# S4D convolution with a gated feed-forward layer: one of the multiplies that build the taps goes from VectorE to GpSimd, and the planner's rules and numbers change

## The chip, the cores and the metric

The kernel runs on one core of a Trainium2 chip. A core has TensorE (PE in the tables; PEld is its weight load), VectorE (DVE), ScalarE (ACT), GpSimd (POOL) and SyncE (SP), which here issues nearly all DMAs. The engines run side by side, each through its own instructions in a fixed order, and wait for each other by semaphores. SBUF is the on-chip memory that all of them work on; PSUM is the small memory that TensorE writes and that VectorE and ScalarE read. The metric is the device time of one execution in microseconds (us).

## The reference

Two branches over the same input `u` of 2048 positions by 640 channels are mixed by a gate. Branch A is a state-space layer: for each channel a kernel `K` of 2048 taps is a sum over 128 complex exponentials, and `u` is convolved with it (by an FFT in the reference). Branch B is a feed-forward layer with 1728 hidden units.

```python
def _A_ref(u, log_A_real, A_imag, C_real, C_imag, log_dt, D_skip):
    dt = jnp.exp(log_dt)
    A = -jnp.exp(log_A_real) + 1j * A_imag
    C = (C_real + 1j * C_imag) * dt[:, None]
    P = jnp.exp((A * dt[:, None])[:, :, None] * pos[None, None, :])
    K = 2.0 * jnp.einsum("dn,dnl->dl", C, P).real
    ...
    y = jnp.fft.irfft(Uf * Kf[None, :, :], L2)[:, :, :L]
    return y + u * D_skip[None, None, :]

def _B_ref(x, w1, w2):
    h = jnp.maximum(jnp.einsum("bsd,df->bsf", x, w1), 0)
    return jnp.einsum("bsf,fd->bsd", h, w2)

g = _sigmoid((x * gate_w).sum(-1, keepdims=True))
return g * a + (1 - g) * b
```

## The kernel before

**The branches.** The feed-forward layer runs as single-pass float32 matmuls of split operands (a high and a low half, `w1h`/`w1l`, `hh`/`hl`), into PSUM banks named `pf`, in three parts of the hidden units. The state-space layer has three stages: parameters (small vector work on 128x640 tables), generation of the taps, and the convolution as a two-level transform with matmuls into banks named `pc`. The feed-forward matmuls fill TensorE between the matmuls of the other branch through the whole run.

**Generation.** The 640 channels go in 40 chunks of 16, and two chunks make a pair. For a chunk of 128 states by 16 channels:

- TensorE multiplies the chunk's parameters with small tables into the only `pg` buffer (`products`, `pe`). The columns are phases in turns and logarithms of magnitudes, 64 of each per channel: 32 fine steps and 32 coarse ones.
- ScalarE rounds the phases to integers (`whole`, the CAST `sc<-pg`) and takes Exp of the magnitudes (`exps`, `mg<-pg`), VectorE subtracts the rounded phase (`sc<-pg,sc`) and clears the sign (`sc<-sc`, TENSOR_SCALAR), and ScalarE takes the Sine and the Cosine (`sc<-sc`, `sc<-sc,half_pi`). The subtraction is what frees `pg`, together with Exp.
- GpSimd sets a column of the magnitudes and extends them by one multiply of 128x512 (`long`: MEMSET `mg`, TENSOR_TENSOR `mg<-mg`).
- `factors` makes the factors of the tap matmuls by four multiplies: parts 0 and 1 (`G<-mg,sc`, 128x512 each), part 2 (`mg<-mg,sc`, 128x1024) and part 3 (`sc<-sc,mg`, 128x1024), which multiplies the fine sines and cosines, in place, by the fine magnitudes. All four read two tiles of SBUF.

The pair then goes through 64 small matmuls into `pk` (`taps`; the trace counts each as two), a transposition on VectorE (`kt<-pk`), a small addition on GpSimd (`kt<-kt,dsk`) and four stores. ScalarE takes the pair's steps in a fixed order, with a table load at each change between Exp and Sine.

**What sets the order.** The program isn't written in the order in which it runs. Each step is a task `A(engine, queue, duration, function, dependences, ...)` with a rank. `Plan.run` then plays the engines forward with the given durations: each engine takes, of the heads of its queues, the one that is ready with the lowest priority number. The priority is the rank plus a number from the table `moves`, by the task's index. The functions are called in the order so found, and `Pinned` keeps each engine's instructions in that order. So durations, rules and table change nothing but the order of instructions on every engine. `run` also counts blocks of 128 matmul instructions on TensorE: a block can begin only some time (`FETCH`, and more by `BUSY` while DMAs are under way) after the one before it. `port=True` lets a VectorE task take up to a quarter longer while the plan has GpSimd busy.

All the instructions go through one helper, so every row of the trace has the line 416; rows are told apart by tile names.

Of the kernel before, what the change touches and what calls it, by code (L numbers as in the profile page):

```python
# [133 lines left out]
def moves():  # L134
    r = {}
    for v, s in (
# [128 lines left out]
class Plan:  # L265
# [3 lines left out]
    CHANGE = dict(PE=0.15, ACT=1.3)  # L269
    HOLD = .1  # L270
    FETCH = 3.2
    BUSY = 0.4
    WAITS = 1.0095
    STALL = 3.0
    SLACK = .4
# [1313 lines left out]
```

## Time and profile before

| | us |
|---|---|
| median of 3 runs (673.36 to 676.02) | 673.42 |
| the profiled execution | 671.55 |
| its span, first to last instruction | 669.8 |
| VectorE busy | 535.4 |
| TensorE busy | 613.2 |
| ScalarE busy | 376.8 |
| GpSimd busy | 148.0 |

The granted clock of TensorE is 0.977 of full speed. In the profile's rows a group is `engine operation out<-in shapes xcount | busy us, mean ns | idle us just before, and what ended it`. A row in order of time begins with its start and its duration in us. "issue" is time in which an engine waited for nothing that the trace shows. A row of a tile gives shortest, median and longest duration in ns. A busy TensorE is not one at its peak, since its matmuls overlap.

### The profile page before, as it was taken

Reading aid. Unit: us, or ns where it says so; the run is one execution under the profiler, and the core shown is the slowest. Engines: PE = TensorE matmul, PEld = TensorE weight load, DVE = VectorE, ACT = ScalarE, POOL = GpSimd, SP = SyncE. Lnnn points to the kernel's source line nnn. Section 1 sums busy time; section 2 is a strip of 40 time slices with the busy share of each in tenths; the row PEclk is TensorE's granted clock in tenths of the full one; section 3 lists DMA queues with packets and bytes.
Section 4 is the critical chain, followed back from the end, with each engine's and each line's share of the span. In section 5 each row is a group of like instructions: output and inputs, shape, how many; then the busy total and the mean of one; then the engine's idle time right before and its main releaser. Section 6 shows DMA issues by size and latency. Waiting matters only on the chain.

```text
span 669.8 us, 19196 instructions
## 1 busy us (share of the span) xinstructions
PE 613.2 (92%) x8196; PEld 481.6 (72%) x8196; DVE 535.4 (80%) x778; ACT 376.8 (56%) x535; POOL 148.0 (22%) x213
## 2 busy tenths in 40 slices
PE   7988988898998999999999987997999997799985
PEld 6988978897886988987978866653675544546673
DVE  4899849999999899998989892987678676678441
ACT  5446378886998678887787860050532522333422
POOL 0000011112112222221322210050520621522633
PEclk9999999998999899998999997999999997999998
DMA  9955844232455552641742468654057837046345
GB/s 245 320 184 190 258 155 146 68 144 97 126 161 158 214 171 56 233 125 37 249 134 57 138 140 296 157 171 101 13 193 216 198 111 221 23 116 181 80 137 117
DMA packets 76302, 102.76 MB, mean 153 GB/s; under 512 B 7609, under 2 KB 59449, under 8 KB 75962
## 3 DMA queue, kind: packets, MB, share of 16 engines
q1 hardware_dynamic: 76058, 101.14, 50.2%
q8 instruction: 64, 1.05, 0.7%
q10 hardware_dynamic: 160, 0.41, 0.3%
q14 instruction: 20, 0.16, 0.1%
HBM read 62.33 MB, written 39.19 MB: 152 GB/s over the span
## 4 chain that ended last, share of the span: by engine, by line
PE 50%; DVE 20%; issue 11%; ACT 7%; DMA 6%; SPq 2%; POOL 2%; POOLq 0%; DVEq 0%; ACTq 0%
PE pf L416 33%; PE pc L416 10%; PE pk L416 5%; DVE sc L416 5%; ACT sc L416 3%; DVE G L416 3%; SPq L416 2%; PE pg L416 2%; DMA y__84<-yo 2%; DVE mg L416 2%; DVE ku L416 2%; DMA xu<-in_A_u_dram 2%; ACT mg L416 1%; POOL ku L416 1%; DVE hl L416 1%
## 5 line engine op out<-in xcount | busy, mean ns | idle before, releaser
L416 PE MATMUL pf<-xx,w1h 128*128 128x256 f32 (+1 forms) x760 | 190.1, 347 | 3.8 <-issue 1.3
L416 PEld LDWEIGHTS pf<-xx,w1h 128*128 128x128 f32 x760 | 124.8, 192 | 37.3 <-issue 22.2
L416 PE MATMUL pf<-xx,w1l 128*128 128x512 f32 (+1 forms) x340 | 117.1, 345 | 0.1
L416 PE MATMUL pf<-w2h,hh 128*128 128x320 f32 x288 | 91.2, 320 | 3.0 <-DVE q L416 1.5
L416 POOL TENSOR_TENSOR mg<-mg 128x512 f32<-128x512 f32 x40 | 51.9, 1298 | 177.1 <-ACT mg L416 177.1
L416 PE MATMUL pf<-w2l,hh 128*128 128x320 f32 x288 | 88.4, 311 | 0.0
L416 DVE STREAM_TRANSPOSE ku<-pc 128x512 f32<-128x512 f32 x80 | 76.1, 1061 | 6.3 <-PE pc L416 6.2
L416 ACT COPY ku<-pc 128x512 f32<-128x512 f32 (+1 forms) x60 | 43.7, 748 | 60.3 <-PE pc L416 60.1
L416 POOL TENSOR_TENSOR ku<-ku,kx 128x256 f32<-128x256 f32 x80 | 56.2, 736 | 92.9 <-DVE ku L416 69.8
L416 PE MATMUL pf<-w2h,hl 128*128 128x320 f32 x256 | 75.4, 318 | 0.8 <-DVE hl L416 0.8
L416 PEld LDWEIGHTS pf<-xx,w1l 128*128 128x128 f32 x340 | 65.3, 192 | 9.4 <-issue 1.5
L416 PEld LDWEIGHTS pf<-w2h,hh 128*128 128x128 f32 x288 | 54.6, 190 | 12.0 <-issue 5.2
L416 ACT CAST sc<-pg 128x1024 int32<-128x1024 f32 x40 | 40.5, 1012 | 39.8 <-PE pg L416 39.8
L416 DVE TENSOR_TENSOR sc<-pg,sc 128x1024 f32<-128x1024 f32 x40 | 48.7, 1217 | 9.6 <-ACT mg L416 9.3
L416 ACT ACT_TABLE_LOAD x42 | 53.9, 1283 | 2.7 <-PE pk L416 2.0
L416 PEld LDWEIGHTS pf<-w2l,hh 128*128 128x128 f32 x288 | 54.7, 190 | 0.2
L416 PEld LDWEIGHTS pf<-w2h,hl 128*128 128x128 f32 x256 | 46.9, 190 | 7.6 <-issue 6.1
L416 DVE TENSOR_TENSOR mg<-mg,sc 128x1024 f32<-128x1024 f32 x40 | 50.5, 1262 | 2.3
L416 ACT ACTIVATE hh<-pf 128x512 fp32r<-128x512 f32 (+1 forms) x40 | 20.4, 509 | 53.7 <-PE pf L416 53.6
L416 DVE TENSOR_TENSOR sc<-sc,mg 128x1024 f32<-128x1024 f32 x40 | 49.5, 1238 | 0.0
L416 PE MATMUL pc<-ku,tm 64*32 64x256 f32 x1280 | 43.4, 397 | 6.4 <-issue 4.2
L416 DVE STREAM_TRANSPOSE ku<-ku 128x512 f32<-128x512 f32 x40 | 25.5, 685 | 25.9 <-ACT ku L416 25.9
(165 smaller groups left out, 1182.2 us busy)
## 6 DMA issues: line engine op xcount, KB each, us to landing
xx<-xt SPq DMA_DIRECT2D x24, 640.0 KB, 5.5
xt<-xx SPq DMA_DIRECT2D x16, 640.0 KB, 5.5
part<-q SPq DMA_DIRECT2D x16, 640.0 KB, 3.4
q<-part SPq DMA_DIRECT2D x16, 640.0 KB, 4.3
ws<-in_B_w_dram SPq DMA_DIRECT2D x20, 320.0 KB, 3.9
kd<-kt SPq DMA_DIRECT2D x80, 64.0 KB, 1.8
ck<-kd SPq DMA_DIRECT2D x40, 128.0 KB, 2.8
xu<-in_A_u_dram SPq DMA_DIRECT2D x10, 512.0 KB, 5.9
```

What stands on the lines that cost most here:

```text
L416: return lambda *a, **k: self._tc.keep_in_program_order(f(*a, **k))
```

## The change

Part 3 of `factors` runs on GpSimd. In the planner, a VectorE, ScalarE or GpSimd task that follows one of its own engine that it depends on begins 0.11 later than it did (`RAW`); the request for a block of matmul instructions is made 24 instructions ahead of the block's start (`AHEAD`, through `when`), and no earlier than the task's dependences; `FETCH` and `BUSY` are larger. A number of durations are smaller, no task has `port=True` any more, and the table of `moves` is another one.

```diff
     for v, s in (
-            (-3.36, "588-683/5"),
+            (-2.99, "2"),
...
-    FETCH = 3.2
-    BUSY = 0.4
+    FETCH = 3.55
+    BUSY = 0.5
+    AHEAD = 24
+    RAW = 0.11
...
-                r = max(r, d.end - d.lag if d.eng == t.eng else d.end)
+                r = max(r, d.end - d.lag + (self.RAW if d.eng in ('DVE', 'ACT', 'POOL') else 0) if d.eng == t.eng else d.end)
...
+        def block():
+            return asked + self.FETCH + self.BUSY * min(12.0, max(0.0, dma - asked))
+
+        def when(c):
+            for (t0, a), (t1, b) in zip(ran[-2::-1], ran[:0:-1]):
+                if a <= c:
+                    return t0 + (t1 - t0) * (c - a) / (b - a) if b > a else t1
+            return 0.0
...
-                done += self.WAITS * t.n
+                w = self.WAITS * t.n
+                ran += [(start + change, total), (self.free[e], total + w)]
+                done, total = done + w, total + w
                 while done >= 128:
                     done -= 128
-                    at = self.free[e] - t.dur * min(1, done / t.n)
-                    self.free[e] += max(0, block - at)
-                    at = max(at, block)
-                    block = at + self.FETCH + self.BUSY * min(8.0, max(0.0, dma - at))
+                    c, at, b = total - done, self.free[e] - t.dur * min(1, done / w), block()
+                    if b > at:
+                        self.free[e] += b - at
+                        ran[-1:] = [(at, c), (b, c), (self.free[e], total)]
+                        at = b
+                    asked = min(at, max(known, when(c - self.AHEAD)))
...
-            y = A('POOL', 'm', 1.6, long, [x], use=[m_], rank=1)
+            y = A('POOL', 'm', 1.15, long, [x], use=[m_], rank=1)
...
                         x = st.pop(('s2', c))[:, :, :, :32]
-                        V.tensor_mul(x, x, m[:, None, :, 65:97].to_broadcast([128, 2, C, 32]))
+                        P.tensor_mul(x, x, m[:, None, :, 65:97].to_broadcast([128, 2, C, 32]))
...
             for k, dep in enumerate(((ex, sn), (ex, sn), (ex, cs), (me, sn, cs))):
-                fs.append(A('DVE', 'g4', 1.2 if k > 1 else 0.62, part(k), dep, take=[g_] if k == 0 else (),
-                            use=[w['s'], w['m']] + ([g_] if k == 1 else []), rank=G4R, port=True))
+                if k == 3:
+                    fs.append(A('POOL', 'f', 2.15, part(k), dep, use=[w['s'], w['m']], rank=G4R))
+                    break
+                fs.append(A('DVE', 'g4', 1.14 if k > 1 else 0.6, part(k), dep, take=[g_] if k == 0 else (),
+                            use=[w['s'], w['m']] + ([g_] if k == 1 else []), rank=G4R))
```

VectorE in the middle of the generation, at one pair of chunks, before (the numbers tell tiles apart: `sc_3360` and `sc_3405` are the two chunks' phases and sines, `sc_3547` belongs to the next pair; `q` is the feed-forward layer's sum, read from PSUM):

```order
L416 STREAM_TRANSPOSE kt_3507<-pk_3426 128x8x2x32
L416 SCALAR_TENSOR_TENSOR G_3513<-mg_3369,sc_3360 128x16x32
L416 TENSOR_TENSOR q_3121<-pf_3410,q_3121 128x320
L416 TENSOR_TENSOR G_3513<-mg_3369,sc_3360 128x16x32
L416 TENSOR_TENSOR mg_3369<-mg_3369,sc_3360 128x16x2x32
L416 TENSOR_TENSOR q_3121<-pf_3516,q_3121 128x320
L416 TENSOR_TENSOR sc_3360<-sc_3360,mg_3369 128x32x32
L416 SCALAR_TENSOR_TENSOR G_3563<-mg_3422,sc_3405 128x16x32
L416 TENSOR_TENSOR q_3121<-pf_3541,q_3121 128x320
L416 TENSOR_TENSOR G_3563<-mg_3422,sc_3405 128x16x32
L416 TENSOR_TENSOR sc_3547<-pg_3498,sc_3547 128x1024
```

And the same pair of chunks' place in the changed kernel (`sc_3293` and `sc_3341` are the pair, `sc_3464` the next pair's first chunk), as far as the next pair's subtraction:

```order
L444 STREAM_TRANSPOSE kt_3425<-pk_3343 128x8x2x32
L444 SCALAR_TENSOR_TENSOR G_3428<-mg_3302,sc_3293 128x16x32
L444 TENSOR_TENSOR G_3428<-mg_3302,sc_3293 128x16x32
L444 TENSOR_TENSOR q_2944<-pf_3334,q_2944 128x320
L444 TENSOR_TENSOR mg_3302<-mg_3302,sc_3293 128x16x2x32
L444 SCALAR_TENSOR_TENSOR G_3462<-mg_3408,sc_3341 128x16x32
L444 TENSOR_TENSOR q_2944<-pf_3438,q_2944 128x320
L444 TENSOR_TENSOR G_3462<-mg_3408,sc_3341 128x16x32
L444 TENSOR_TENSOR mg_3408<-mg_3408,sc_3341 128x16x2x32
L444 TENSOR_TENSOR q_3115<-pf_3466,q_3115 128x320
L444 TENSOR_TENSOR sc_3464<-pg_3415,sc_3464 128x1024
```

The multiplies `sc<-sc,mg` are gone from VectorE, and both chunks' `mg<-mg,sc` now stand ahead of the next pair's subtraction; before, the second chunk's followed it. One pair later VectorE has:

```order
L444 SCALAR_TENSOR_TENSOR G_3630<-mg_3478,sc_3464 128x16x32
L444 TENSOR_TENSOR G_3630<-mg_3478,sc_3464 128x16x32
L444 TENSOR_TENSOR mg_3478<-mg_3478,sc_3464 128x16x2x32
L444 TENSOR_TENSOR q_3115<-pf_3622,q_3115 128x320
L444 SCALAR_TENSOR_TENSOR G_3655<-mg_3589,sc_3577 128x16x32
L444 TENSOR_TENSOR G_3655<-mg_3589,sc_3577 128x16x32
L444 TENSOR_TENSOR mg_3589<-mg_3589,sc_3577 128x16x2x32
L444 TENSOR_TENSOR sc_3657<-pg_3617,sc_3657 128x1024
```

The order of the steps is the same, with one `q` among them. GpSimd in the changed kernel, at the first of these two pairs:

```order
L444 MEMSET mg_3302 128x16
L444 TENSOR_TENSOR mg_3302<-mg_3302 128x16x32
L444 MEMSET mg_3408 128x16
L444 TENSOR_TENSOR mg_3408<-mg_3408 128x16x32
L444 TENSOR_TENSOR kt_3425<-kt_3425,dsk_119 128x8
L444 TENSOR_TENSOR sc_3293<-sc_3293,mg_3302 128x32x32
L444 TENSOR_TENSOR sc_3341<-sc_3341,mg_3408 128x32x32
```

The last two rows are new there; before, the `kt` addition was followed by the next pair's MEMSET. TensorE at the start of the first block of the convolution, before (`pc<-ku,tm` are the small matmuls, `pf` the feed-forward ones):

```order
L416 MATMUL pc<-ku,tm 32x256 x48
L416 MATMUL pf<-xx,w1h_4513 128x512 x2
L416 MATMUL pf<-xx,w1l_4514 128x512
L416 MATMUL pc<-ku,tm 32x256 x32
L416 MATMUL pf<-xx,w1h_4513 128x512 x2
L416 MATMUL pf<-xx,w1l_4514 128x512
L416 MATMUL pc<-ku,tm 32x256 x48
```

and in the changed kernel:

```order
L444 MATMUL pc<-ku,tm 32x256 x48
L444 MATMUL pf<-xx,w1h_4418 128x512 x2
L444 MATMUL pf<-xx,w1l_4419 128x512
L444 MATMUL pc<-ku,tm 32x256 x16
L444 MATMUL pf<-xx,w1h_4418 128x512 x2
L444 MATMUL pf<-xx,w1l_4419 128x512
L444 MATMUL pc<-ku,tm 32x256 x32
L444 MATMUL pf<-xx,w1h_4418 128x512 x2
L444 MATMUL pf<-xx,w1l_4419 128x512
L444 MATMUL pc<-ku,tm 32x256 x32
```

The same 128 small matmuls stand in four runs where there were three.

More of the change, by code (lines that the diff above doesn't have):

```diff
@@ L268 @@
     LAG = dict(PE=0.22, DVE=0.12, ACT=0.12, POOL=0.1, SP=0.0, PY=0.0)
-    CHANGE = dict(PE=0.15, ACT=1.3)
+    CHANGE = dict(PE=0.12, ACT=1.3)
     HOLD = .1
-    FETCH = 3.2
-    BUSY = 0.4
+    FETCH = 3.55
+    BUSY = 0.5
+    AHEAD = 24
+    RAW = 0.11
     WAITS = 1.0095
@@ L332, in run @@
         self.free = {e: 0.0 for e in self.LAG}
-        mode, dma, log, done, block = {}, 0.0, [], 34.0, 3.0
+        mode, dma, log, done, total, asked, ran = {}, 0.0, [], 34.0, 34.0, -1.0, [(0.0, 34.0)]
         heads = {k: 0 for k in self.queues}
+        def block():
[5 more added lines that the diff above has]
+            return 0.0
         while True:
@@ L356, in key @@
                     if e == 'PE' and done + t.n >= 128:
-                        k += self.STALL * max(0.0, block - at - t.dur * (128 - done) / t.n)
+                        k += self.STALL * max(0.0, block() - at - t.dur * (128 - done) / t.n)
                     return k
@@ L373, in run @@
             _, e, t, start = best
+            known = self.ready(t)[0]
             change = self.CHANGE.get(e, 0) if t.mode is not None and mode.get(e) not in (None, t.mode) else 0
@@ L381, in run @@
             if e == 'PE':
-                done += self.WAITS * t.n
+                w = self.WAITS * t.n
+                ran += [(start + change, total), (self.free[e], total + w)]
+                done, total = done + w, total + w
                 while done >= 128:
                     done -= 128
-                    at = self.free[e] - t.dur * min(1, done / t.n)
-                    self.free[e] += max(0, block - at)
-                    at = max(at, block)
-                    block = at + self.FETCH + self.BUSY * min(8.0, max(0.0, dma - at))
+                    c, at, b = total - done, self.free[e] - t.dur * min(1, done / w), block()
[4 more added lines that the diff above has]
+                    asked = min(at, max(known, when(c - self.AHEAD)))
+                del ran[:-400]
             if t.port:
@@ L575, in logits @@
                 else:
-                    self.zs.append(A('DVE', 'z', 0.85, lambda t=t: go(t), dep, use=[s_], rank=LOGR))
+                    self.zs.append(A('DVE', 'z', 0.74, lambda t=t: go(t), dep, use=[s_], rank=LOGR))
         def trans(g, third, src):
@@ L842, in gates @@
             for k in range(17):
-                a = [A('DVE', 'gate', 0.2, rec.one(k, 17, go), a, rank=4)]
+                a = [A('DVE', 'gate', 0.16, rec.one(k, 17, go), a, rank=4)]
             self.gated = a[0]
@@ L1168, in long @@
                 P.tensor_mul(m[:, :, :32], m[:, :, 63:31:-1], m[:, :, 33:34].to_broadcast([128, C, 32]))
-            a = visit[c] = A('PE', None, 0.24, pe, [rd, opened, *self.tg_done], take=[p_], use=[r_], rank=GPR, mode='r', n=4)
+            a = visit[c] = A('PE', None, 0.28, pe, [rd, opened, *self.tg_done], take=[p_], use=[r_], rank=GPR, mode='r', n=4)
             b = acts[c, 0] = A('ACT', None, 0.97, whole, [a], take=[s_], use=[p_], rank=2)
@@ L1173, in products @@
                   use=[p_, s_], rank=G1R)
-            y = A('POOL', 'm', 1.6, long, [x], use=[m_], rank=1)
+            y = A('POOL', 'm', 1.15, long, [x], use=[m_], rank=1)
             o = A('DVE', 'g1', 0.62, lambda: V.tensor_scalar(I(st['sc', c][1]), I(st['sc', c][0]), 0x7fffffff, None,
-                                                             op0=ALU.bitwise_and), [d], use=[s_], rank=G1R, port=True)
+                                                             op0=ALU.bitwise_and), [d], use=[s_], rank=G1R)
             h = TWO_PI
@@ L1357, in stage1 @@
                 self.plan.join([pes[kind, i, q - 1], a])
-            ts = [A('DVE', 's' + kind, 1.04, turn(h), [a], use=[b_, buf], rank=SKD if k else SUD)
+            ts = [A('DVE', 's' + kind, 0.95, turn(h), [a], use=[b_, buf], rank=SKD if k else SUD)
                   for h in range(2)]
@@ L1428, in inv2 @@
                 gs = range(t * 4 // TURNS, (t + 1) * 4 // TURNS)
-                vs.append(A('PE', None, 1.76 / TURNS, lambda gs=gs: pe(gs), [*dep, tn] + vs[-1:], take=() if t else bs,
+                vs.append(A('PE', None, 1.8 / TURNS, lambda gs=gs: pe(gs), [*dep, tn] + vs[-1:], take=() if t else bs,
                             use=[K[i]] + (list(bs) if t else []), rank=S2P, mode='c', n=128 // TURNS))
@@ L1436, in relay @@
             d = slice(r * 8, r * 8 + 8)
-            return A('DVE', 'rl', 0.7, lambda: V.transpose(out=st['Y', i][:, :, d].rearrange("p b e f -> p e f b"),
+            return A('DVE', 'rl', 0.6, lambda: V.transpose(out=st['Y', i][:, :, d].rearrange("p b e f -> p e f b"),
                                                            in_=st['X', i][:, :, d].rearrange("p g e f -> p e f g")),
@@ L1472, in inv1 @@
                     self.plan.join([pes['4', i, b0 - 4], a])
-                c = A('ACT', 's4', 1.24, copy, [a], take=[x for x in (y_, g_ if first else None) if x],
+                c = A('ACT', 's4', 1.0, copy, [a], take=[x for x in (y_, g_ if first else None) if x],
                       use=[b_] + ([g_] if g_ and not first else []), rank=S4A)
```

219 rows, old and new, of the table r are left out of this document.

## The prediction

> **What bounds the kernel now.** I read the page's span, then the stages, then the groups of instructions by shape, and last the order of time of single instructions on VectorE (DVE), ScalarE (ACT) and GpSimd (POOL). Times below are of one profiled execution, which took 671.55 us with a span of 669.8; the median of the three runs is 673.42, so a sum made on the span is carried over as a difference, and the median gets the same difference.
>
> ```profile
> span 669.8 us, 19196 instructions
> ```
>
> ```profile
> core 0: us, PE busy (x) PEld busy (x) DVE busy (x) ACT busy (x) POOL busy (x), PEclk, DMA share, GB/s
> ...
> 111.00:408.00 297.00, 277.77 (x3961) 239.83 (x3960) 273.86 (x366) 233.48 (x266) 59.90 (x91) 0.98 0.44 142
> 408.00:670.00 262.00, 236.65 (x3525) 148.59 (x3524) 175.22 (x245) 81.52 (x164) 82.65 (x107) 0.96 0.51 140
> ```
>
> Parameters and the first pair of chunks come ahead of 111 us; then the other 19 pairs, and from 408 us the convolution. The change works on the 19 pairs, 297 us or 15.6 us a pair: DVE is busy 273.86 of it, so it idles 23.1, and PE idles 19.2. POOL is busy in a fifth of it. That is the case for handing POOL some of DVE's work, and the rest of this text is about what such a hand-over costs.
>
> ```profile
> L416 POOL TENSOR_TENSOR ku<-ku,kx 128x256 f32<-128x256 f32 x80 | 56.2, 736 | 92.9 <-DVE ku L416 69.8 <-PE pc L416 22.1 <-DMA yj<-part 0.7
> L416 DVE TENSOR_TENSOR mg<-mg,sc 128x1024 f32<-128x1024 f32 x40 | 50.5, 1262 | 2.3
> L416 DVE TENSOR_TENSOR sc<-sc,mg 128x1024 f32<-128x1024 f32 x40 | 49.5, 1238 | 0.0
> L416 POOL TENSOR_TENSOR yo<-yo,yj 128x512 f32<-128x512 f32 x8 | 10.2, 1285 | 33.5 <-ACT yo L416 28.3 <-issue 5.3
> L416 ACT ACTIVATE hh<-pf 128x512 fp32r<-128x512 f32 x24 | 14.3, 595 | 45.9 <-PE pf L416 45.9
> ...
> L416 POOL TENSOR_TENSOR mg<-mg x40: 1041/1109/2036, 90.0 to 385.0; 128x512 f32<-128x512 f32 x40
> ...
> L416 DVE TENSOR_TENSOR G<-mg,sc x40: 670/684/696, 97.4 to 398.5; 128x512 f32<-128x512 f32 x40
> L416 DVE TENSOR_TENSOR mg<-mg,sc x40: 1207/1225/2080, 98.2 to 399.2; 128x1024 f32<-128x1024 f32 x40
> ```
>
> Of the groups, the third is what moves: 40 multiplies, one a chunk. The last three rows give shortest, median and longest time in ns. The stage has one POOL multiply a chunk already: 1041 undisturbed, 2036 at worst. DVE's `mg` multiply is 1225 in the median and 2080 at worst. Those spreads are the first hint.
>
> **The shared resource.** In order of time, DVE's and POOL's rows at three places:
>
> ```profile
> 200.47 1.22 DVE L416 TENSOR_TENSOR sc<-sc,mg 128x1024 f32<-128x1024 f32 x1
> 201.60 1.67 DVE L416 TENSOR_TENSOR w2l<-ws,w2h 128x640 fp32r<-128x640 f32 x1
> ...
> 200.84 1.75 POOL L416 TENSOR_TENSOR mg<-mg 128x512 f32<-128x512 f32 x1 [6.17 <-ACT mg L416]
> ...
> 302.19 2.08 DVE L416 TENSOR_TENSOR mg<-mg,sc 128x1024 f32<-128x1024 f32 x1
> ...
> 302.14 1.05 POOL L416 TENSOR_TENSOR mg<-mg 128x512 f32<-128x512 f32 x1 [4.73 <-ACT mg L416]
> ...
> 251.65 1.22 DVE L416 TENSOR_TENSOR sc<-pg,sc 128x1024 f32<-128x1024 f32 x1
> ...
> 251.69 1.05 POOL L416 TENSOR_TENSOR mg<-mg 128x512 f32<-128x512 f32 x1 [3.54 <-ACT mg L416]
> ```
>
> At 302.14 POOL starts first and takes its 1.05; DVE's multiply, 0.05 behind it, takes 2.08 against its median of 1.23, so it lost 0.85, nearly all that POOL had left. At 200.84 POOL comes while a DVE multiply runs to 201.69: POOL takes 1.75, that is, it ends 0.90 after DVE's end, and the next DVE instruction, queued at 201.60, in turn takes 1.67. So a DVE instruction whose inputs both lie in SBUF and a POOL multiply exclude each other, and whoever asked first goes first. A DVE instruction that reads PSUM isn't touched: at 251.65 the subtraction takes its 1.22 and POOL beside it its 1.05. Today POOL's multiply often falls beside just this, since both wait for the same Exp.
>
> **The multiply off DVE.** DVE issues its next instruction before the record of the last one ends, so what is saved is the spacing:
>
> ```profile
> 271.70 0.48 DVE L416 TENSOR_TENSOR q<-pf,q 128x320 f32<-128x320 f32 x1
> 272.10 1.22 DVE L416 TENSOR_TENSOR sc<-sc,mg 128x1024 f32<-128x1024 f32 x1
> 273.23 0.69 DVE L416 SCALAR_TENSOR_TENSOR G<-mg,sc 128x512 f32<-128x512 f32 x1
> ...
> 274.93 1.23 DVE L416 TENSOR_TENSOR sc<-pg,sc 128x1024 f32<-128x1024 f32 x1
> ```
>
> 273.23 - 272.10 = 1.13 us, 40 times: 45.2 us less on DVE.
>
> **The multiply on POOL.** No row has POOL at 128x1024. From below, twice the undisturbed 1041 is 2.08. From above, 736 at 256 elements and 1285 at 512 rise by 549 per 256, which at 1024 gives 1285 + 1098 = 2.38. The operands are nearest to the second (two full streams), yet the first is the same stage; I take the middle, 2.23, an estimate. The new multiply waits for the Sine and the Cosine of its chunk, which is just when DVE starts that chunk's three multiplies `G`, `G`, `mg`, all with both inputs in SBUF. In the two pairs shown of the new order only `q` instructions, which read PSUM, stand among them. So each new multiply gets the port after the running DVE instruction and the next one waits. By the row at 200.84 the port is held for the duration less 0.15, so 2.08; a `q` behind which DVE needn't wait covers its spacing of 0.40 (272.10 - 271.70). Two `q` stand in the first pair, one in the second, and a pair has two new multiplies: 0.3 each, and I allow 0.40. Lost: 2.08 - 0.40 = 1.68, times 40 = 67.2 us.
>
> Net on DVE: 67.2 - 45.2 = +22. With POOL at 2.08 it is +16, at 2.38 +28. DVE's idle 23.1 us of the stage are waits for ACT and PE; some holds will fall into these, and I give them a quarter, 6 us: **+16**.
>
> How long POOL holds the port for a long instruction is the open price. The rows show only 1.05-us instructions; were the port given back after as much as they hold, each new multiply would cost DVE 0.85 as at 302.19, 34 in all, and the net would be -11. The Trainium skill, page "SBUF — State Buffer", section "Who interferes with whom", states that whoever issues first gets the shared pair "for the whole instruction" and the other fully blocks. The rows above agree for 1.05 us; none here shows 2.2. By that rule the net stays +22 before the idle time, and the case of -11 is out. I keep that case as a rival.
>
> **What is late next.** PE has only one `pg` buffer, so each second chunk's matmuls wait for DVE's subtraction of the first:
>
> ```profile
> 266.25 1.28 ACT L416 ACT_TABLE_LOAD   x1
> ...
> 273.85 1.04 ACT L416 ACTIVATE mg<-pg 128x1024 f32<-128x1024 f32 x1
> 277.03 1.02 ACT L416 CAST sc<-pg 128x1024 int32<-128x1024 f32 x1 [2.14 <-PE pg L416]
> 277.94 1.04 ACT L416 ACTIVATE mg<-pg 128x1024 f32<-128x1024 f32 x1
> 279.01 1.28 ACT L416 ACT_TABLE_LOAD   x1
> ```
>
> Here the subtraction starts at 274.93, at once after Exp's end (274.89), and ACT waits 2.14 for the next chunk. In the new order both chunks' multiplies stand ahead of the subtraction, so a blocked DVE delays it, then PE, then ACT. I take that as part of the +16, not on top; as a rival it counts alone. The pair's `pk` matmuls on PE now wait for POOL as well; its second multiply asks for the port ahead of DVE's second `mg`, so it ends first and that wait costs nothing, unless the `kt` addition ahead of it in POOL's queue is late, and then up to one multiply, 2.2 us a pair. Queued on POOL behind the new multiplies are only the small `kt` addition and the next pair's `mg` multiply; the store of `kt` has two buffers and its reader is the convolution, so I cost that at nothing; without that cover it is one POOL multiply, 2.2 us, at the last pair.
>
> **The scheduler's recount.** It adds no instruction; it moves rows on every queue, SyncE's included. That the parameters' instructions and some feed-forward matmuls now stand ahead of the first chunk costs nothing by itself: it is the same DVE and PE work, taken from later pairs. Where PE waited for nothing that the trace shows:
>
> ```profile
> PE pc L416 <- issue: 12.1, 5, 4.2
> PE pk L416 <- issue: 4.2, 1, 4.2
> ```
>
> Those 16.3 us in six waits are behind runs of small matmuls, mostly in the convolution, and the new order breaks such runs with feed-forward matmuls. Between -12 (nearly all gone) and +8 (half as much again elsewhere) I take **-3**, since much of it only moves to another wait.
>
> **Sum.** +16 - 3 = +13: profiled 684.5, median 673.4 + 13 = **686**.
>
> **Rivals.** (a) The new multiplies fall beside PSUM readers and into DVE's waits, or the port comes back early: price -11 for the multiplies and -3, 659 us. It decides itself at a loss of 1.13 us a multiply, where DVE's saving is used up: 0.95 of the 2.08 has to be covered. For it: DVE and POOL have the time, and POOL is 80% idle in the stage. Against: both wait for the same Sine. PE's 19.2 us of idle time and the issue waits cap it near 650. (b) The ring is what decides, every pair: the subtraction comes 2 x 1.68 = 3.4 later than the 274.93 of the rows, since one removed multiply and one `mg` that now stands ahead of it even out; the pair of 279.01 - 266.25 = 12.76 becomes 16.1, with two evacuations of feed-forward banks on ACT at 0.6 (the `hh` group) 17.3, against 15.6 now: 19 x 1.7 = 32, 705 us. For it: ACT works in a fixed order. Against: some pairs have slack elsewhere. (c) Hold and saving cancel, or the order happens to even it out: 670 to 677.
>
> **Chances.** Under 0.5% (3.4 us) this kernel's measurement tells nothing. My forecast, 677 to 697 by the ends of the POOL price and of the recount: 0.52. Rival (b), above that: 0.16. Rival (a), under 670: 0.24. (c): 0.08. So slower 0.68, same 0.08, faster 0.24. The range over all cases, which leaves out some 0.06 at the far end of (a) and 0.06 at that of (b), is 653 to 708.
>
> **What would show it.** Right: DVE's `mg<-mg,sc` and `G` get medians well over 1225 and 684 ns, with maxima near 3.3 us (1.23 + 2.08) and 2.8, POOL's `sc<-sc,mg` a median above its shortest, the wait of ACT for `pg` grows from 2 us a pair, and 19 pairs take more than 297 us. Wrong: the `mg` mean stays near 1.25, the pairs shorten towards 14 us and PE has no idle time left. If the stage is shorter by some us and the whole isn't, the convolution's order gave it back.

## The result, and the profile after

The changed kernel takes 745.21 us (median of 4 runs, 742.09 to 748.61) against 673.78 us for the kernel before (also 4 runs), a ratio of 1.105 with a 95% interval of 1.099 to 1.111: 71 us slower. The direction was predicted, the size was not: 686 was forecast, with a range over all cases up to 708.

The span on the page of the changed kernel, and then busy time by stage (columns as in the prediction's table of stages: ahead of the first pair's taps, the 19 pairs, the convolution):

```profile
span 741.6 us, 19212 instructions
```

```profile
0.00:118.00 118.00, 107.46 (x785) 103.77 (x785) 85.11 (x168) 59.70 (x109) 8.22 (x14) 0.99 0.70 214
118.00:485.00 367.00, 289.93 (x3886) 247.19 (x3886) 312.55 (x326) 236.62 (x263) 156.50 (x132) 0.91 0.35 112
485.00:742.00 257.00, 237.32 (x3525) 146.66 (x3525) 173.23 (x245) 81.79 (x164) 83.09 (x107) 0.98 0.52 142
```

The first stage is 7 us longer than before, the convolution 5 us shorter, and the 19 pairs take 367 us where they took 297: 19.3 us a pair instead of 15.6. Nearly all of the loss is there. VectorE (DVE) is busy 312.6 us of it, 38.7 more than before, although it does 40 multiplies less. It idles 54.5 us, where it idled 23.1: 31.4 more. Both parts together are the 70 us. TensorE's idle time in the stage grew from 19.2 to 77 us, and its granted clock in this stage fell from 0.98 to 0.91.

The groups of instructions that grew, by shape (the first row is ScalarE's group in the kernel before), and the shortest, median and longest time of four of them:

```profile
L416 ACT CAST sc<-pg 128x1024 int32<-128x1024 f32 x40 | 40.5, 1012 | 39.8 <-PE pg L416 39.8
...
L444 POOL TENSOR_TENSOR sc<-sc,mg 128x1024 f32<-128x1024 f32 x40 | 108.1, 2715 | 48.3 <-ACT sc L444 47.8 <-PE pf L444 0.2
L444 DVE TENSOR_TENSOR mg<-mg,sc 128x1024 f32<-128x1024 f32 x40 | 87.8, 2195 | 3.7 <-DVE G L444 0.5
L444 DVE SCALAR_TENSOR_TENSOR G<-mg,sc 128x512 f32<-128x512 f32 x40 | 59.2, 1480 | 3.7 <-ACT sc L444 3.6
L444 DVE TENSOR_TENSOR G<-mg,sc 128x512 f32<-128x512 f32 x40 | 38.4, 960 | 0.0
...
L444 ACT CAST sc<-pg 128x1024 int32<-128x1024 f32 x40 | 40.4, 1010 | 95.1 <-PE pg L444 95.0
```

```profile
L444 DVE SCALAR_TENSOR_TENSOR G<-mg,sc x40: 649/693/2724, 107.5 to 474.2; 128x512 f32<-128x512 f32 x40
...
L444 DVE TENSOR_TENSOR G<-mg,sc x40: 672/684/2694, 108.1 to 476.8; 128x512 f32<-128x512 f32 x40
L444 POOL TENSOR_TENSOR sc<-sc,mg x40: 2238/2604/3218, 108.8 to 473.1; 128x1024 f32<-128x1024 f32 x40
L444 DVE TENSOR_TENSOR mg<-mg,sc x40: 1207/2377/3271, 109.3 to 477.6; 128x1024 f32<-128x1024 f32 x40
```

The multiply on GpSimd (POOL) takes 2.24 us undisturbed. DVE's `mg` has a median of 2377 ns in place of 1225, and the longest, 3.27, is 1.23 + 2.04 us. The two `G` still have their old medians, but single ones take 2.7 us: which of the three is hit varies. ScalarE (ACT) waits 95 us for `pg` in all, where it waited 39.8.

One pair in order of time shows how this becomes idle time of the other engines. Rows of DVE, POOL, TensorE (PE) and ACT of the changed kernel:

```profile
286.32 3.08 DVE L444 TENSOR_TENSOR mg<-mg,sc 128x1024 f32<-128x1024 f32 x1
289.33 2.69 DVE L444 SCALAR_TENSOR_TENSOR G<-mg,sc 128x512 f32<-128x512 f32 x1
291.94 1.53 DVE L444 TENSOR_TENSOR G<-mg,sc 128x512 f32<-128x512 f32 x1
293.57 1.23 DVE L444 TENSOR_TENSOR mg<-mg,sc 128x1024 f32<-128x1024 f32 x1
294.71 0.68 DVE L444 SCALAR_TENSOR_TENSOR gw<-pf,xu 128x512 fp32r<-128x512 f32 x1
...
296.53 1.21 DVE L444 TENSOR_TENSOR sc<-pg,sc 128x1024 f32<-128x1024 f32 x1
...
285.83 5.64 POOL L444 TENSOR_TENSOR sc<-sc,mg 128x1024 f32<-128x1024 f32 x2 [2.68 <-ACT sc L444]
291.41 0.13 POOL L444 MEMSET mg<- 128x16 f32 x1
291.55 1.37 POOL L444 TENSOR_TENSOR mg<-mg 128x512 f32<-128x512 f32 x1
...
288.97 0.46 PE L444 MATMUL pf<-w2h,xu 128*128 128x320 f32 x2
295.45 0.64 PE L444 MATMUL pf<-w2h,gw 128*128 128x320 f32 x1 [6.02 <-DVE gw L444]
...
299.55 0.50 PE L444 MATMUL pg<-tg,PS 32*128 32x512 f32 x4
...
300.15 1.01 ACT L444 CAST sc<-pg 128x1024 int32<-128x1024 f32 x1 [8.68 <-PE pg L444]
```

Three times running, a DVE instruction is stuck behind POOL: 3.08 for 1.23, 2.69 for 0.68, 1.53 for 0.68, 4.7 us in all. The first two stand behind the new multiplies, the third behind the 128x512 multiply that POOL had before, too, and that now comes after the new ones. Behind them on DVE stands `gw<-pf,xu`, a piece of the feed-forward layer that has nothing to do with the port (as the prediction calls what the two engines share), since it reads PSUM. PE needs it and stands still for 6.02 us. PE's `pg` matmuls are queued behind those feed-forward matmuls and come at 299.55, and so ACT waits 8.68. PE's waits for DVE in the 19 pairs, as the sum in us, the number and the longest, first one row of the kernel before and then those of the changed one:

```profile
PE pg L416 <- DVE sc L416: 2.3, 3, 1.4
...
PE pk L444 <- DVE mg L444: 21.7, 8, 5.1
PE pf L444 <- DVE q L444: 13.0, 6, 3.8
PE pf L444 <- DVE gw L444: 10.0, 2, 6.0
PE pf L444 <- DVE hl L444: 7.3, 4, 3.1
PE pf L444 <- DVE xu L444: 6.9, 2, 4.4
...
PE pg L444 <- DVE sc L444: 4.8, 3, 2.7
```

All of PE's waits for DVE in this stage come to 72.7 us; before they came to 12.3. Of the 72.7, 21.7 are taps' matmuls waiting for a blocked `mg`, 37.2 (13.0 + 10.0 + 7.3 + 6.9) are feed-forward pieces, and only 4.8 are the subtraction that frees `pg`.

After its standstill PE is also slow for a while. The stages table again, in 2-us slices around it (the third number from the end is the granted clock):

```profile
292.00:294.00 2.00, 0.00 (x0) 0.00 (x0) 1.90 (x3) 0.00 (x0) 0.98 (x2) 0.52 1.02 410
...
296.00:298.00 2.00, 2.00 (x9) 2.00 (x8) 1.84 (x3) 0.00 (x0) 0.00 (x0) 0.50 0.02 10
...
300.00:302.00 2.00, 2.00 (x87) 1.81 (x86) 0.15 (x1) 1.85 (x2) 0.00 (x0) 1.00 0.01 4
```

Idle from 289.4, PE has half its clock from 292.1 to 298.9; of these 6.8 us the last 3.5, from 295.45 on, have work. The Trainium skill, page "TensorE: Matmul & The Clock Gate", section "What's actually happening", states such a rule: after an idle window of some 3.4 us the array runs at half clock, and gets the full one back after about as much sustained work. For the way back these rows agree, with 3.5 us of work at half clock; the fall came sooner, 2.7 us after the last matmul ended. So this wait of 6.0 us costs more than itself: by an estimate from the 3.5 us at half clock, some 1.7 us more. In the whole trace PE stands still for over 3 us 13 times, against 3 times before.

### The profile page after: what moved, and what is told of

It reads as the page before. It is cut to its first block, busy times and chain, and to the rows that moved or that the text cites. A ratio compares the mean times of both kernels' runs of the same rounds, so it can differ in the third digit from the quotient of the medians.

```text
span 741.6 us, 19212 instructions
## 1 busy us (share of the span) xinstructions
PE 634.7 (86%) x8196; PEld 497.6 (67%) x8196; DVE 570.9 (77%) x738; ACT 378.1 (51%) x535; POOL 247.8 (33%) x253
## 5 line engine op out<-in xcount | busy, mean ns | idle before, releaser
L444 PE MATMUL pf<-xx,w1h 128*128 128x256 f32 (+1 forms) x760 | 194.4, 353 | 14.6 <-DVE hl L444 7.3
L444 PEld LDWEIGHTS pf<-xx,w1h 128*128 128x128 f32 x760 | 127.1, 196 | 52.3 <-issue 23.5
L444 POOL TENSOR_TENSOR sc<-sc,mg 128x1024 f32<-128x1024 f32 x40 | 108.1, 2715 | 48.3 <-ACT sc L444 47.8
L444 PE MATMUL pf<-xx,w1l 128*128 128x512 f32 (+1 forms) x340 | 119.0, 350 | 0.1
L444 PE MATMUL pf<-w2h,hh 128*128 128x320 f32 x288 | 92.9, 326 | 13.7 <-DVE q L444 13.0
L444 POOL TENSOR_TENSOR ku<-ku,kx 128x256 f32<-128x256 f32 x80 | 56.6, 739 | 104.5 <-DVE ku L444 82.5
L444 DVE TENSOR_TENSOR mg<-mg,sc 128x1024 f32<-128x1024 f32 x40 | 87.8, 2195 | 3.7 <-DVE G L444 0.5
L444 POOL TENSOR_TENSOR mg<-mg 128x512 f32<-128x512 f32 x40 | 47.5, 1186 | 106.2 <-ACT mg L444 105.2
L444 PE MATMUL pk<-mg,sc 128*32 128x64 f32 x1280 | 51.2, 252 | 30.9 <-DVE mg L444 21.7
L444 PEld LDWEIGHTS pk<-mg,sc 128*32 128x32 f32 x1280 | 42.5, 131 | 37.0 <-issue 36.7
L444 DVE SCALAR_TENSOR_TENSOR G<-mg,sc 128x512 f32<-128x512 f32 x40 | 59.2, 1480 | 3.7 <-ACT sc L444 3.6
L444 PEld LDWEIGHTS pf<-w2h,hl 128*128 128x128 f32 x256 | 47.8, 194 | 11.1 <-issue 10.9
```

What stands on the lines that cost most here:

```text
L444: return lambda *a, **k: self._tc.keep_in_program_order(f(*a, **k))
```

## The experiments

Each expectation weighs two theories of its own. In e1, e2 and e5, A says that POOL's reading shuts DVE's instructions with two SBUF inputs out, and that this is the loss; B says that POOL's longer way, or an order that doesn't fit, is. All ratios are to the kernel before, run on the same chip. The chips differ: the kernel before has medians from 669.41 to 673.78 on them, so a difference between two runs of different chips is uncertain by some us.

| run | us | ratio (95%) |
|---|---|---|
| e1, changed kernel, POOL only fills | 653.73 | 0.972 (0.964 to 0.980) |
| e2, changed kernel, POOL reads one input | 673.07 | 1.001 (0.997 to 1.005) |
| e3, the recount alone | 722.68 | 1.075 (1.069 to 1.082) |
| e4, the multiply alone | 743.64 | 1.106 (1.098 to 1.114) |
| e5, as e4, POOL only fills | 659.10 | 0.981 (0.978 to 0.984) |
| e6, subtraction ahead of the second `mg` | 737.68 | 1.096 (1.089 to 1.103) |
| e7, POOL's multiply after the last `mg` | 771.24 | 1.148 (1.144 to 1.152) |
| e8, old table for the taps, new for the convolution | 693.31 | 1.031 (1.026 to 1.036) |
| e9, as e7, ahead of POOL's next `mg` | 769.38 | 1.148 (1.142 to 1.154) |
| e10, POOL's multiply half as long | 683.21 | 1.018 (1.013 to 1.023) |
| e11, POOL's multiply in four pieces | 706.40 | 1.055 (1.048 to 1.061) |
| e12, new rules, old table, multiply on DVE | 679.27 | 1.016 (1.011 to 1.021) |

**e1 and e5: what if POOL reads nothing?** In the changed kernel:

```diff
-                        P.tensor_mul(x, x, m[:, None, :, 65:97].to_broadcast([128, 2, C, 32]))
+                        P.memset(x, 0.5)
+                        P.memset(x, 0.5)
```

> The changed kernel in its own order, with GpSimd's multiply of the sines replaced by two fills of the same tile, so GpSimd has an instruction in the same place but reads nothing (the multiplication is left out). Theory A, the shared port: VectorE's multiplies with two inputs in SBUF are held up only by a GpSimd instruction that reads SBUF. Then VectorE's mg and G medians go back to about 1.23 and 0.68 us, ScalarE's wait for the pg buffer falls from 95 us to 40 or less, and the time falls from 745 to 645 to 670. Theory B, the long way round: GpSimd is an extra engine between Sine and the tap matmuls and the new order is simply a bad one. Then most of the loss stays: 720 to 745.

Measured: 653.73 us (two runs, 650.51 and 656.96). ACT's wait for `pg` is 35.2 us. The tile's rows, one place in order of time, and the 19 pairs in e1:

```profile
L444 POOL MEMSET sc<- x80: 951/956/966, 108.5 to 385.3; 128x1024 f32 x80
...
L444 DVE TENSOR_TENSOR mg<-mg,sc x40: 1207/1226/1229, 109.0 to 385.2; 128x1024 f32<-128x1024 f32 x40
```

```profile
270.51 1.23 DVE L444 TENSOR_TENSOR mg<-mg,sc 128x1024 f32<-128x1024 f32 x1
...
270.11 3.96 POOL L444 MEMSET sc<- 128x1024 f32 x4 [2.35 <-ACT sc L444]
```

```profile
114.50:393.40 278.90, 264.38 (x3888) 228.03 (x3888) 230.09 (x325) 235.60 (x263) 121.02 (x170) 0.99 0.45 147
```

POOL is busy at the same places, with two fills of 0.96 us where the multiply took 2.24, and DVE isn't touched: no `mg` is over 1229 ns. The changed kernel less this one is 91.5 us, more than the whole loss, and theory A has its numbers. The stage also shows what the multiply's removal from DVE is worth when nothing blocks: DVE has 44 us less to do than before (230.1 against 273.9), and the stage is 18 us shorter (279 against 297). The rest became DVE's idle time, which is 49 us where it was 23. PE is busy 264.4 of the 279, so it is likely the next bound; no run tests that.

Set against e1, the stage of the changed kernel is 88.1 us longer (367.0 against 278.9). DVE is busy 82.5 us longer in it and idles only 5.7 us more (54.5 against 48.8). So most of the 31.4 us by which DVE's idle time grew over the kernel before comes with the multiply's leaving, and the loss itself is nearly all time in which DVE is blocked.

The same two fills in the order of before (on top of e4's edit, below):

> The planner and table of before, part 3 as a GpSimd task, and in the place of the multiply two fills of the same 128x1024 elements, which read nothing; the multiplication by the fine magnitudes is left out. It differs from the kernel with the multiply alone (743.6 us) only in what GpSimd reads. Theory A (GpSimd's reading blocks VectorE, and nearly all of the loss comes from that in the old order too): VectorE's mg and G are back at 1.23 and 0.68 us, and since VectorE is 45 us lighter than before, 640 to 675 us. Theory B (the old table doesn't fit a multiply on GpSimd, and that is what costs): 715 to 745 us whatever GpSimd reads.

The 19 pairs in e5, and then in e4, which has the multiply itself:

```profile
105.00:387.00 282.00, 269.50 (x3951) 234.25 (x3952) 232.65 (x331) 233.48 (x266) 120.24 (x170) 0.99 0.41 137
...
107.00:473.00 366.00, 298.02 (x3952) 256.32 (x3953) 311.35 (x331) 233.47 (x264) 155.61 (x132) 0.92 0.31 105
```

659.10 us. Here too DVE gets 41 us lighter and the stage 15 us shorter. Between e4 and e5, which have one table and differ in what POOL does, lie 84.5 us; in the stage it is 84.0, of which DVE is busy 78.7 and idle 5.3. Theory A holds in both orders; what POOL's reading costs hardly depends on the planner's table.

**e2: one input instead of two.**

```diff
-                        P.tensor_mul(x, x, m[:, None, :, 65:97].to_broadcast([128, 2, C, 32]))
+                        P.tensor_scalar(x, x, 0.5, None, op0=ALU.mult)
```

> As the run with fills, but GpSimd multiplies the sines by a constant: one stream is read from SBUF, in place (the multiplication by the magnitudes is left out). Theory A: any read of SBUF by GpSimd takes the port; the instruction is perhaps 1.1 to 2.2 us long, and the longest mg multiplies on VectorE are about 1.2 us plus that. If it is as long as the real multiply the time stays at 730 to 750, if half as long 690 to 715. Theory B: like the fills, 720 to 745, with VectorE's medians at 1.23 and 0.68.

Measured: 673.07 us, as before the change and in neither theory's range. The tile's rows, and DVE and POOL in order of time:

```profile
L444 POOL TENSOR_SCALAR sc<-sc x40: 2763/2968/3813, 108.5 to 403.4; 128x1024 f32<-128x1024 f32 x40
L444 DVE TENSOR_TENSOR mg<-mg,sc x40: 1208/1870/2060, 108.9 to 404.0; 128x1024 f32<-128x1024 f32 x40
```

```profile
282.12 1.87 DVE L444 TENSOR_TENSOR mg<-mg,sc 128x1024 f32<-128x1024 f32 x1
284.32 0.67 DVE L444 SCALAR_TENSOR_TENSOR G<-mg,sc 128x512 f32<-128x512 f32 x1
284.92 1.52 DVE L444 TENSOR_TENSOR G<-mg,sc 128x512 f32<-128x512 f32 x1
286.54 1.23 DVE L444 TENSOR_TENSOR mg<-mg,sc 128x1024 f32<-128x1024 f32 x1
...
281.74 5.88 POOL L444 TENSOR_SCALAR sc<-sc 128x1024 f32<-128x1024 f32 x2 [2.37 <-ACT sc L444]
```

The instruction with one input is the longer one on POOL, 2.97 us, and costs DVE far less: a kernel whose POOL works longer at the same place is 72 us faster. So POOL's longer way is not what costs. Two of them run from 281.74 to 287.62. DVE's `mg` at 282.12 is 0.65 late and ends at 283.99, inside the first one; the next `G` isn't late at all; the `G` at 284.92 meets the second one's beginning and is 0.84 late; the `mg` at 286.54 runs beside the second at its usual 1.23. In all 39 rows of `mg` and `G` that are late in e2, DVE goes on 0.9 to 1.4 us after POOL's instruction began. So this instruction shuts DVE out for something like its first us only. For a one-input instruction the rule that was weighed in the prediction ("for the whole instruction", the Trainium skill, page "SBUF — State Buffer", section "Who interferes with whom") doesn't hold in these rows. For the two-input multiply it does: in all 54 rows of `mg` and `G` that are late in the changed kernel, DVE goes on 0.13 to 0.15 us before the end of a POOL multiply's record, and the longest loss is 2.04 us.

**e4 and e3: each half of the change alone.** e4 is the kernel before with the two edits

```diff
+                if k == 3:
+                    fs.append(A('POOL', 'f', 2.15, part(k), dep, use=[w['s'], w['m']], rank=G4R))
+                    break
...
-                        V.tensor_mul(x, x, m[:, None, :, 65:97].to_broadcast([128, 2, C, 32]))
+                        P.tensor_mul(x, x, m[:, None, :, 65:97].to_broadcast([128, 2, C, 32]))
```

and e3 the changed kernel with their reverse.

> The kernel before with the multiply on GpSimd (a GpSimd task of 2.15 in the plan), with the old count, durations and table. Theory A: the loss is the multiply's, whatever the planner: 710 to 760, with mg and G medians on VectorE as in the changed kernel. Theory B: the recount is what costs, so 665 to 690.

> The changed kernel with the multiply back on VectorE (a VectorE task of 1.14 in the plan); the recount of instruction blocks and waits, the durations and the new table of priorities stay. Theory A: no contention beyond that of before, so 665 to 690: the stage of the 19 pairs is near 297 us again and the convolution near the changed kernel's 257. Theory B, that the new order is at fault: 700 or more, with PE and ScalarE waiting as in the changed kernel.

The multiply alone costs as much as the whole change, 743.64 against 745.21: theory A of e4. The recount alone gave 722.68, some 50 us slower than before; that is outside e4's theory B and e3's theory A and inside e3's theory B. Its 19 pairs:

```profile
119.70:451.50 331.80, 290.62 (x3987) 251.29 (x3983) 280.01 (x370) 236.31 (x263) 61.41 (x92) 0.95 0.39 129
```

DVE is hardly blocked here (its `mg` has a median of 1225 ns) and little busier than before, 280 us against 274; it idles 52. The new order is a bad one for a DVE that has the multiply.

**e12 and e8: rules or table?** Both have the multiply on DVE and the new rules and durations; e12 has the table of before (`moves`), e8 the table of before (`moves0`) up to the taps and the new one behind:

```diff
-MOVES = moves()
+MOVES = {**{k: v for k, v in moves0().items() if k < 1775}, **{k: v for k, v in moves().items() if k >= 1775}}
```

> The multiply on VectorE as before, the new rules and durations of the planner, and the table of before throughout; against the kernel before only the rules and durations differ, against the recount alone (722.7 us) only the table. No work is left out. Theory A (the new table, made for a VectorE without the multiply, is what costs 50 us there): 668 to 685 us. Theory B (the rules themselves put the instructions in a bad order, and no table is to blame): 700 to 725 us.

> The multiply on VectorE as before; the new rules and durations of the planner; the table of before for the tasks up to the taps and the new table for those of the convolution. No work is left out. The changed kernel's last stage (the convolution) was 5 us shorter than before, and its issue waits fell from 12.1 to 7.5 us. Theory A (the recount helps the convolution and its table for the taps only fits a VectorE without the multiply): 662 to 672 us, with 12 to 16 us a pair in the taps. Theory B (the recount's rules themselves spoil the taps' order): 690 to 725 us, as the recount alone (722.7).

e12 took 679.27, in theory A's range: of the recount's 50 us some 10 are the rules and durations, and the new table is the rest. e8 took 693.31, which lies in its theory B's range, but e12 has the same rules and takes over 10 us less, so the rules are not all that costs. The convolution's part of the new table is no gain by itself: the convolution was 5 us shorter than before in the changed kernel, it is 8 us longer in e8, and with the old table throughout, in e12, it takes 256.5 us, 5.5 shorter.

**e10 and e11: shorter holds.** e10 multiplies one half and fills the other; e11 does the whole multiply in four instructions of 128x256:

```diff
-                        P.tensor_mul(x, x, m[:, None, :, 65:97].to_broadcast([128, 2, C, 32]))
+                        P.tensor_mul(x[:, 0], x[:, 0], m[:, :, 65:97])
+                        P.memset(x[:, 1], 0.5)
```

```diff
-                        P.tensor_mul(x, x, m[:, None, :, 65:97].to_broadcast([128, 2, C, 32]))
+                        for u in range(2):
+                            for v in (0, 8):
+                                P.tensor_mul(x[:, u, v:v + 8], x[:, u, v:v + 8], m[:, v:v + 8, 65:97])
```

> The changed kernel, with GpSimd multiplying the fine sines only (128x512) and filling the fine cosines' half; the cosines' magnitudes are left out. GpSimd's reading instruction is half as long, near 1.05 us against 2.24 at the shortest. With nothing read the time was 653.7, with the whole multiply 745.2. Theory A (VectorE is in the path all along, and every us held counts): half of the 91.5 us, 695 to 705 us, with mg at up to 1.23 + 1.05 = 2.3 us. Theory B (the stage has slack that takes the first part, and the ring starts to count only above it): 660 to 685 us.

> The changed kernel, with the multiply in four instructions of 128x256 one behind the other on GpSimd; no work is left out. Theory A (the port is held for a whole instruction and is given to who asked first, so VectorE gets in between the pieces): VectorE's mg and G end at most 0.75 us late (mg up to 2.0), while GpSimd's pieces wait in turn, and the time is 690 to 730 us. Theory B (a GpSimd that has the next piece queued keeps the port through all four): mg up to 3.3 us as before and 740 to 765 us.

POOL's row and DVE's longest group in e10, then in e11:

```profile
L444 POOL TENSOR_TENSOR sc<-sc,mg x40: 1203/1250/2261, 107.1 to 415.3; 128x512 f32<-128x512 f32 x40
```

```profile
L444 DVE TENSOR_TENSOR mg<-mg,sc 128x1024 f32<-128x1024 f32 x40 | 63.9, 1598 | 3.7 <-DVE G L444 0.5
```

```profile
L444 POOL TENSOR_TENSOR sc<-sc,mg x160: 682/1146/1727, 108.9 to 443.1; 128x256 f32<-128x256 f32 x160
...
L444 DVE TENSOR_TENSOR mg<-mg,sc x40: 1210/1538/1716, 111.7 to 441.0; 128x1024 f32<-128x1024 f32 x40
```

In e11 no `mg` exceeds 1716 ns: DVE gets in between two pieces (theory A), and an `mg` loses at most 0.5 where it lost 2.0. POOL in turn waits for DVE (median 1146 against 682 undisturbed), and is longer in all, 4 x 0.68 = 2.7 us. The kernel is 39 us faster than the changed one and still 5% slower than before.

What DVE lost in each, from its groups `mg`, `G`, `G` (and the sign clear in e11), less the same groups of e1:

| | DVE's loss, us | time over e1, us |
|---|---|---|
| e1 | 0 | 0 |
| e2 | 24.9 | 19.3 |
| e10 | 37.3 | 29.5 |
| e11 | 43.9 | 52.7 |
| changed kernel | 81.6 | 91.5 |

Up to 37 us lost, a part is absorbed: in e10's 19 pairs DVE idles 41 us where it idles 49 in e1. Theory B of e10 (some slack first) is nearer, at 683.2. From e10 to the changed kernel 44 us more of loss cost 62. In e11 the pieces also make PE's taps wait for POOL, 16.1 us, so it lies above the line of the others.

**e6, e7 and e9: other places for the same work.** e6 puts the next pair's first subtraction ahead of the second chunk's `mg`, e7 and e9 put POOL's multiplies behind the pair's last `mg`; e9 alone has the `prio` line, by which they come ahead of the next pair's multiply on POOL.

```diff
+        for c in range(1, n - 1, 2):
+            tasks[c]['f'][2].deps += (tasks[c + 1]['d'],)
```

```diff
+        for c in range(n):
+            tasks[c]['f'][3].deps += (tasks[c | 1]['f'][2],)
+            tasks[c]['f'][3].prio = -5
```

> The changed kernel, with one dependence more in the plan: the second chunk's mg multiply on VectorE comes after the next pair's first subtraction, which frees the only pg buffer. No work is left out. In the changed kernel that subtraction starts some 5 us after its inputs are there, behind blocked multiplies. Theory A1 (the ring through pg passes VectorE's loss on, and can be shortened): the subtraction comes 1.2 to 3.2 us earlier in each of the 19 pairs, ScalarE's wait for pg falls from 95 to under 70 us, and the time to 700 to 730 us. Theory A2 (VectorE's queue itself is the bound, the ring only one of its outlets): the wait for pg falls, but others take its place; 738 to 755 us.

> The changed kernel, with GpSimd's two multiplies of a pair held back in the plan until VectorE has done the pair's last mg multiply, so that they run beside the subtractions and the feed-forward sums, which read PSUM. No work is left out. Theory A: what VectorE loses falls from some 85 us to between 25 and 50, the taps' matmuls come up to 4.5 us later but have slack, and the time is 680 to 725 us. Theory B (the taps wait for the multiply and no slack is there): 740 to 780 us, with TensorE's pk waiting for GpSimd.

> As the run with the multiplies held back behind the pair's last mg multiply (771.2 us), but with the two multiplies ahead of the next pair's MEMSET and mg multiply in GpSimd's order, where they stood behind them. No work is left out. Theory A (in that run the multiplies came late only because GpSimd had to wait for the next pair's Exp first): they now run beside the subtractions and sums that read PSUM, VectorE loses 30 to 50 us, and the time is 680 to 725 us. Theory B (a pair's taps have no slack for two multiplies of 2.2 us after VectorE's last one): 735 to 775 us.

e6 took 7.5 us less than the changed kernel, which is hardly clear of noise (the intervals of the two ratios overlap): ACT's wait for `pg` fell from 95.0 to 86.1, and PE now waits for the subtraction itself,

```profile
PE pg L444 <- DVE sc L444: 33.6, 12, 5.4
```

which is nearer to A2 than to A1. e7 and e9 are slower still, in theory B's ranges, though not in the way that it had: PE waits only 0.9 and 1.5 us for POOL. DVE loses 58 and 68 us there in place of 82, but in part at another place, in the sign clear, which stands between the subtraction and the Sine (e9):

```profile
L444 DVE TENSOR_SCALAR sc<-sc x40: 643/694/2760, 102.3 to 484.2; 128x1024 int32<-128x1024 int32 x40
```

```profile
PE pg L444 <- DVE sc L444: 45.9, 16, 10.9
```

PE's wait for the subtraction is 45.9 us there, and the TensorE clock over the whole run 0.926. Each of these orders also went through a table that wasn't made for it, and how much of their 771 and 769 us is due to that was not separated. No version here that computes the whole result beats the kernel before.

## Why the prediction was right in direction and wrong in size

**The shared resource: right.** That a two-input POOL multiply and DVE's two-input instructions exclude each other was the main argument, and e1 and e5 show it: the same kernels without POOL's reading are 91.5 and 84.5 us faster. The direction is no luck, since it comes from this.

**The multiply on POOL: right in size.** 2.23 was estimated, 2.24 is the shortest. The hold was put at 2.08 and the longest `mg` shows 2.04.

**The loss by the new multiplies: nearly right.** 67.2 us were forecast, 1.68 a multiply, with 0.40 of each hold covered by `q`. In the changed kernel 38 rows of `mg` and `G` end with a new multiply; they lose 70.8 us, 1.77 for each of the 40. The cover works where it is there: with a `q` just ahead 7 of 8 rows lose only 1.61 to 1.65, and without one all but two lose 1.80 to 2.04. But a `q` stands just ahead of 8 rows alone, and the 0.40 for each was an allowance without a reason: the 0.3 that the prediction counted from the order would have given 71.2.

**POOL's old multiply: a term put at nothing.** The prediction named the 128x512 multiply as queued behind the new ones and gave it no cost. Before, it often fell beside the subtraction, which reads PSUM; now it falls beside `G` and `mg`, 16 of which end with it and lose 10.9 us. Before, DVE's multiplies lost 2.5 us to it. Both kinds together are the 81.6 us of the table above (38.8 + 31.8 + 11.0 by groups).

**The multiply off DVE: the step that failed most.** 45.2 us less on DVE is right (44 in the stage of e1), but the sum set it in full against the loss, as if DVE alone were the stage. Where nothing blocks, e1's stage is only 18 us shorter and e5's 15, and the whole kernels gain some 17 to 19 and 13. PE's limit stood in the text of rival (a), as a cap "near 650", and wasn't applied to the term of the sum.

**The idle time: failed too.** A quarter of DVE's 23.1 us was to absorb 6 us of holds. Against e1, DVE's idle time didn't shrink by the holds but grew by 5.7.

**What is late next: the sum nearly right, the way not.** The text named the subtraction and `pg`, "as part of the +16, not on top". On top of DVE's own loss there are only these 5.7 us. But PE waits 4.8 us for the subtraction, 21.7 for a blocked `mg` and 37.2 for feed-forward pieces that stand behind blocked instructions on DVE. e6, which shortens the way that the prediction named, gains 7.5 us, hardly clear of noise. Rival (b) was nearer with 705, and it too counted only the subtraction.

**The recount: not contradicted for this kernel.** -3 was taken between -12 and +8. With the multiply on POOL it measures +1.6 (745.21 against e4's 743.64), and without reading -5.4 (e1 against e5); both are within the intervals. That it would cost 50 us with the multiply left on DVE wasn't foreseen.

In the 19 pairs the forecast was -45.2 + 67.2 - 6 = +16. Measured, the same three terms are -18.1 (e1 against before), +82.5 (DVE's busy time, changed kernel against e1) and +5.7 (its idle time), +70. These add up by construction, as differences of three traces; what they show is where the 54 us between forecast and result lie: 27 in what the removal is worth, 15 in the loss and 12 in the idle time. Why a loss of 37 us is absorbed in part (e10) and one of 82 is not, stays open.

**What would show it.** `mg`'s median and maximum, the maxima of `G`, POOL's median above its shortest, ACT's wait for `pg` and the longer pairs came as named. The medians of `G` did not move.

## What to carry to other kernels

Work taken off an engine may be worth no more than the idle time of the next one: here 44 us less on VectorE shortened a stage by 18, in which TensorE had idled 19.2. Time lost on the engine counted for more: 37 us cost 29.5, and 82 cost all and some more. So the two must not be netted on one engine. Before a GpSimd instruction goes beside VectorE, look at the number of SBUF inputs of both and at the length of the single instruction: fills cost VectorE nothing, one input a part, two inputs nearly their whole length, and four short pieces about half of one long one. Look also at what the new instruction pushes back on its own engine: GpSimd's old multiply, pushed back behind the new ones, cost VectorE 10.9 us where it had cost 2.5. Ask what stands behind a blocked instruction in its queue, unrelated work included: in the changed kernel TensorE missed that more than the step that is next in the data's own chain.

## What the runs showed of the hardware that was not expected

- A GpSimd TENSOR_SCALAR of 128x1024 takes 2.97 us (median), longer than the two-input multiply of the same size (2.24 at the shortest), and delays a VectorE multiply of 128x1024 by 0.65 us (0.83 at most) instead of up to 2.04. Why the port comes back so early is not settled.
- VectorE's TENSOR_SCALAR with its one input in SBUF (`sc<-sc`) can be blocked too: 2760 ns for 694 in e9. Here the Trainium skill, page "SBUF — State Buffer", section "Who interferes with whom", names `tensor_scalar` among those that can take the shared pair, and these rows agree.
- Within 6.0 us without work TensorE's clock fell to half, and stayed so for the first 3.5 us of work behind it; over the 19 pairs the granted clock was 0.91 against 0.99 where nothing was blocked (e1).
